# Zero multiplies on TensorE in the front of a gated recurrence with a feed-forward network: more of them, and narrow ones for the remainders

## The chip, the cores and the metric

The kernel runs on one core of one Trainium2 chip. Its time is the device time in microseconds (us) of one execution. Engines: TensorE (PE in the profile; its weight loads are PEld), VectorE (DVE), ScalarE (ACT), GpSimd (POOL), and SyncE (SP), which issues most of the transfers.

## The reference, cut to what matters

A recurrence over 768 steps for 4 batches and 8 heads of width 48, and on its output, 3072 tokens of 384, a feed-forward network with a hidden width of 1536:

```python
f = 1.0 / (1.0 + np.exp(-f_logit))
for t in range(S):
    state = f[:, :, t, :, None] * state + np.einsum('bhd,bhe->bhde', k[:, :, t], v[:, :, t])
    y[:, :, t] = np.einsum('bhd,bhde->bhe', q[:, :, t], state)
...
gate = np.maximum(x @ w_gate, 0.0)
val = x @ w_val
return (gate * val @ w_out).astype(np.float32)
```

## The kernel before

**Tiling.** The tokens are cut into 12 units of 256 (one batch, two chunks of 128). For each unit the kernel takes the logarithm of the gates (ACT, L546 and L555 or L550), sums it along the chunk with a triangle of ones on PE (L562 to L564), forms the exponentials (ACT, L577, L580, L587), multiplies them into k and q (the "hats", DVE or POOL, L599 and L605), transposes these (on PE with L637 for units 0 to 3, by a DMA transpose L648 later), forms the scores (L662), masks them (ptm, DVE L676, or ACT L671 and POOL L673), forms the states (L727 or L717, then DVE L513 and L517, POOL L520) and the output of each chunk (L760, or L767 and L771), and copies that into xT (L402, L403) or by xn and a DMA transpose (L790). L699 and L703 form the total decay of a unit. Two units make a group of 512 tokens; the feed-forward part runs over groups: gate and value (L811, with wg and wv), relu (ACT L816), product (DVE L823), output (L841, with wo), eviction into osb and a store (L862).

**Order.** Nothing is scheduled at run time. `Plan.add` collects the operations ("ops"), numbered in the order in which they are added; `SEQUENCE` gives each engine its order by these numbers, and `HOMES` gives each of the eight PSUM banks the list of tiles that live in it, one after the other. `Plan.needs` works out which semaphores each op waits for, and `run` (L904) writes the waits and the op, engine by engine. An engine works in its order: whatever stands behind a waiting op waits too. POOL issues the weights' transfers (wg, wv, wo in four slices of three hidden blocks each; L482) among its other ops, SP all other ones (loads L468).

**Zeros.** `warm` (L891) is a matmul of a tile of zeros with itself into a bank that is free at that point; its result is read by nobody. `FILLERS` says which op has how many zeros ahead of it and in which bank. They come after those waits of the op which the zeros themselves need (`op.early` of them: the tile of zeros is written, the former tile in that bank has been read by the other engines; L105 to L107) and before the op's other waits:

```python
if n == op.early:
    count, k = FILLERS.get(op.idx, (0, 0))
    for _ in range(count):
        warm(banks[k])
```

So PE multiplies zeros while the release of the op is still to come. All zeros are 512 columns wide (`WARM`). They stand in the first 19 us; the first real matmul behind the nine first ones is the sum of unit 0. The PE ops of the front in their order, with the line of their matmuls and when the first of them starts in the profiled execution:

| op | what | line | starts at, us | zeros before: count |
|---|---|---|---|---|
| 67, 68 | sums, unit 0 | L563, L564 | 6.11 | 9 |
| 105, 106 | sums, unit 1 | L563, L564 | 7.72 | 3 |
| 83 | transposes of k, unit 0 | L637 | 10.03 | 5 |
| 85 | transposes of q, unit 0 | L637 | 10.97 | 1 |
| 123 | transposes of q, unit 1 | L637 | 12.29 | 2 |
| 87, 90 | scores, unit 0 | L662 | 12.84, 13.30 | 0 |
| 121 | transposes of k, unit 1 | L637 | 13.77 | 0 |
| 95 | states, unit 0 | L727 | 14.49 | 0 |
| 128 | scores, unit 1 | L662 | 15.58 | 2 |
| 93 | decay, unit 0 | L699, L703 | 15.91 | 0 |
| 96 | output, unit 0, first chunk | L760 | 16.57 | 0 |
| 125 | scores, unit 1 | L662 | 16.91 | 0 |
| 99 | output, unit 0, second chunk | L760 | 17.56 | 1 |
| 245 | sums, unit 2 | L563, L564 | 18.35 | 1 |
| 132 | decay, unit 1 | L699, L703 | 18.69 | 0 |
| 134 | states, unit 1 | L727 | 19.61 | 2 |
| 135, 244, 138 | output of unit 1, sums of unit 2 between | L760, L563 | 20.05 | 0 |
| 154, then 146 | gates, group 0 | L811 | 21.35, 21.90 | 0 |

The zeros of a row stand ahead of its first op. An output op runs in rounds of four matmuls on a quarter of the array's columns each; scores use 48 of the array's rows.

Of the kernel before, what the change touches and what calls it, by code (L numbers as in the profile page):

```python
# [38 lines left out]
class Plan:  # L39
# [45 lines left out]
    def follow(self, sequence, homes, banks, warm):  # L85
        self.link()
        tiles = list(dict.fromkeys(t for op in self.ops for t in dict.fromkeys(op.reads + op.writes + op.opens) if isinstance(t, Bank)))
        opener = {t: op for op in self.ops for t in op.opens}
        for bank, home in zip(banks, homes):
            before = None  # L90
            for n in home:
                tile = tiles[n]
                tile.ap = bank
                if before is not None:
                    for o in before.ops:
                        opener[tile].deps[o] = "raw" if o.eng == opener[tile].eng == "ACT" else "war"
                before = tile
        assert sorted(n for home in homes for n in home) == list(range(len(tiles)))
        place = {i: n for n, i in enumerate(sequence["PE"])}
        for i, (_, k) in warm.items():  # L100
            op = self.ops[i]
            after = [n for n, t in enumerate(homes[k]) if place.get(opener[tiles[t]].idx, -1) >= place[i]]
            past = [tiles[t] for t in (homes[k][:after[0]] if after else homes[k])]
            assert not past or all(place[o.idx] < place[i] for o in past[-1].ops if o.eng == "PE")
            op.hot = [d for d in op.deps if "zeros" in d.writes] + [o for o in (past[-1].ops if past else []) if o.eng != "PE"]  # L105
            for o in op.hot:
                op.deps.setdefault(o, "war")  # L107
        order = {e: [self.ops[i] for i in sequence[e]] for e in self.ENGINES}
        assert sorted(i for e in self.ENGINES for i in sequence[e]) == list(range(len(self.ops)))
        free = {r: 0.0 for r in self.ENGINES + ("hw", "sw")}  # L110
        at = {e: 0 for e in self.ENGINES}
        left = len(self.ops)
        while left:
            ready = [(max([free[e]] + [d.end for d in order[e][at[e]].deps]), e) for e in self.ENGINES
                     if at[e] < len(order[e]) and all(d.end is not None for d in order[e][at[e]].deps)]
            if not ready:
                raise RuntimeError("the sequences wait for each other")
            start, e = min(ready)
            op = order[e][at[e]]
            op.start, op.pos = start, at[e]  # L120
            free[e] = start + op.occ
            op.end = start + op.occ + op.lat
            if op.flow is not None:
                free[op.ring] = max(free[op.ring], start + op.lat) + op.flow
                op.end = free[op.ring] + 1.0
            at[e] += 1
            left -= 1
        self.order = order
        return order
# [126 lines left out]
        21, 19, 67, 33, 44, 53, 54, 57, 95, 91, 65, 143, 116, 106, 135, 149, 125, 130, 162, 187, 161, 194, 174, 230, 277, 209, 236, 238, 243,  # L256
        271, 260, 263, 292, 298, 301, 314, 316],
]
FILLERS = {67: (9, 0), 105: (3, 0), 83: (5, 0), 85: (1, 0), 123: (2, 3), 128: (2, 7), 99: (1, 2), 245: (1, 2), 134: (2, 3)}

UNITS = {
# [21 lines left out]
def bass_hgrn2_outer__then__ffn_reglu_kernel(  # L283
# [76 lines left out]
    zeros = sb("zeros", [128, 512], BF16)  # L360
    banks = [nc.alloc_psum_tensor(f"ps{i}", [128, 512], F32) for i in range(8)]
# [3 lines left out]
    gp, ve, sc, te, sy = nc.gpsimd, nc.vector, nc.scalar, nc.tensor, nc.sync  # L365
# [79 lines left out]
    WARM = 512  # L445
# [439 lines left out]

    for n in FILLERS:
        pl.ops[n].reads.append("zeros")
    order = pl.follow(SEQUENCE, HOMES, banks, FILLERS)
    waits = pl.needs()

    def warm(bank):  # L891
        return te.matmul(bank[:, 0:WARM], zeros[:, 0:128], zeros[:, 0:WARM], start=True, stop=True, skip_group_check=True)

    sems = {e: nc.alloc_semaphore(f"e_{e}") for e in ("PE", "ACT", "DVE", "POOL")}
    for e in ("PE", "ACT", "DVE", "POOL"):
        n = 0
# [7 lines left out]
    def run(name, eng):  # L904
        for op in order[name]:
            for n, d in enumerate(waits[op] + [None]):
                if n == op.early:
                    count, k = FILLERS.get(op.idx, (0, 0))
                    for _ in range(count):
                        warm(banks[k])  # L910
                if d is None:
                    break
                if d.sem is not None:
                    eng.wait_ge(d.sem, d.goal)
                else:
                    eng.wait_ge(sems[d.eng], d.val)
            ins = op.emit()
            if op.sem is not None:
                ins.then_inc(op.sem, 16)
            elif op.inc:  # L920
                ins.then_inc(sems[name], 1)

    run("SP", nc.sync)
    nc.scalar.preload_act_table_set("natural_log_exp_and_others")
    run("ACT", nc.scalar)
    run("DVE", nc.vector)
    run("POOL", nc.gpsimd)
    run("PE", nc.tensor)
# [30 lines left out]
```

## Time and profile before

| | |
|---|---|
| runs of the kernel, us | 189.0, 189.06, 189.38; median 189.06 |
| the profiled execution, us | 188.75 |
| its span, first to last instruction, us | 187.2 |
| around the span, us | 1.55 |
| busy, share of the span | PE 96%, PEld 55%, DVE 65%, ACT 65%, POOL 56% |

How to read it: a row of the timeline is a start in us from the span's start, the time that the merged instructions cover together, engine, line, operation, what it writes <- what it reads, its shape, and how many were merged. A bracket is idle time before it and what ended it. Each matmul's duration holds the way through the array as well as the streaming of its columns; in a row of several the matmuls overlap, so a second one starts before the first has ended. A row in "rows x columns" such as 128\*32 names the part of the array in use. Some matmul records can be missing.

### The profile page before, as it was taken

The page shows a single profiled execution, that of the slowest core. Times are in us where ns is not written, and L with a number is a line of the kernel's source. Part 1 is how long each engine was busy: PE and PEld are TensorE (multiplying, and loading weights), DVE is VectorE, ACT ScalarE, POOL GpSimd, SP SyncE. Part 2 cuts the span into 40 slices and gives each one's busy share as a digit, 9 for nine tenths or more (in the row PEclk, how much of TensorE's full clock was granted, in tenths as well). Part 3 has the DMA queues.
Part 4 walks back from the last instruction along what each step waited for, and adds up shares of the span by engine and source line. Part 5 has one row for each costly group of instructions (what it writes and reads, how often), then busy time and mean ns, then how long its engine had stood idle before and what let it go on. Part 6 is the DMA issues. An engine that isn't in the chain of part 4 may idle for free.

```text
span 187.2 us, 4314 instructions
## 1 busy us (share of the span) xinstructions
PE 179.2 (96%) x1670; PEld 103.0 (55%) x1691; DVE 121.5 (65%) x231; ACT 122.3 (65%) x242; POOL 104.8 (56%) x141
## 2 busy tenths in 40 slices
PE   7888999999999999999999899999999999999995
PEld 2345686467677555555655355555545465444564
DVE  4099856988179899788679696766744644336151
ACT  3998997999888798879677744463554640545201
POOL 4559905991976999989918989470970700000000
DMA  5999999979899999999999999834544022003005
GB/s 153 324 325 267 209 204 216 279 128 152 185 315 162 226 305 244 224 178 260 254 252 225 252 238 217 189 65 111 166 81 106 30 42 66 0 0 130 17 25 210
DMA packets 83167, 32.89 MB, mean 176 GB/s; under 512 B 75334, under 2 KB 83148, under 8 KB 83148
## 3 DMA queue, kind: packets, MB, share of 16 engines
q1 hardware_dynamic: 78348, 29.09, 64.2%
q0 software_dynamic: 4800, 3.54, 12.8%
q8 instruction: 13, 0.21, 0.5%
q14 instruction: 6, 0.05, 0.1%
HBM read 25.96 MB, written 4.73 MB: 164 GB/s over the span
## 4 chain that ended last, share of the span: by engine, by line
PE 76%; DMA 12%; SPq 4%; POOL 2%; ACT 1%; issue 1%; DVE 1%; ACTq 0%
PE ps L811 44%; PE ps L841 23%; DMA wv<-in_moe_w_val_dram 5%; DMA out_dram<-osb 4%; SPq L468 4%; PE ps L662 3%; DMA v_in<-in_v_dram 3%; PE ps L760 2%; PE ps L771 1%; PE ps L767 1%; PE ps L717 1%; POOL vpad L403 1%; POOL wg L482 1%; PE ps L562 1%; PE ps L727 0%
## 5 line engine op out<-in xcount | busy, mean ns | idle before, releaser
L823 DVE TENSOR_TENSOR gT<-relu,ps 128x512 bf16<-128x512 bf16 (+1 forms) x84 | 50.5, 625 | 31.9 <-PE ps L811 24.0
L816 ACT ACTIVATE relu<-ps 128x512 bf16<-128x512 f32 (+1 forms) x84 | 42.6, 536 | 26.1 <-PE ps L811 19.2
L811 PE MATMUL ps<-xT,wv 128*128 128x512 bf16 (+1 forms) x244 | 54.8, 348 | 1.7 <-DVE osb L403 0.9
L811 PE MATMUL ps<-xT,wg 128*128 128x512 bf16 (+1 forms) x241 | 54.2, 347 | 0.7 <-issue 0.2
L841 PE MATMUL ps<-wo,gT 128*128 128x384 bf16 (+2 forms) x300 | 51.9, 320 | 0.0
L841 PEld LDWEIGHTS ps<-wo,gT 128*128 128x128 bf16 x300 | 28.5, 98 | 18.9
L811 PEld LDWEIGHTS ps<-xT,wv 128*128 128x128 bf16 x252 | 23.3, 98 | 20.6 <-DVE osb L403 1.1
L811 PEld LDWEIGHTS ps<-xT,wg 128*128 128x128 bf16 x252 | 23.2, 98 | 19.4 <-ACT ptm L671 0.4
L673 POOL TENSOR_TENSOR ptm<-ptm,seen 128x512 bf16<-128x512 bf16 x21 | 24.0, 1155 | 15.2 <-ACT ptm L671 14.6
L605 POOL TENSOR_TENSOR hats<-q_in,expo 64x384 bf16<-64x384 f32 x28 | 27.8, 995 | 8.0 <-DMA q_in<-in_q_dram 6.0
L402 ACT ACTIVATE osb<-ps 128x384 f32<-128x384 f32 (+2 forms) x17 | 7.9, 471 | 19.9 <-PE ps L841 18.3
L605 DVE TENSOR_TENSOR hats<-k_in,ps 64x384 bf16<-64x384 f32 x32 | 17.7, 552 | 4.8 <-DMA k_in<-in_k_dram 2.3
L676 DVE TENSOR_TENSOR ptm<-ps,seen 128x512 bf16<-128x512 f32 x27 | 17.7, 682 | 1.7 <-PE ps L662 1.6
L403 POOL CAST vpad<-v_in 64x384 bf16<-64x384 f32 x28 | 14.1, 502 | 6.3 <-DMA v_in<-in_v_dram 5.0
L520 POOL TENSOR_TENSOR st<-ssum,dec 128x384 bf16<-128x384 f32 x16 | 13.3, 831 | 7.6 <-DMA dec<-rates 6.4
L671 ACT ACTIVATE ptm<-ps 128x512 bf16<-128x512 f32 x21 | 11.9, 596 | 7.1 <-PE ps L662 7.1
L546 ACT ACTIVATE f_in<-f_in 128x768 f32<-128x768 f32 x12 | 10.1, 844 | 2.3 <-DMA f_in<-in_f_logit_dram 2.3
L580 ACT ACTIVATE expo<-ps 128x384 f32<-128x384 f32 x22 | 10.0, 490 | 2.5 <-DVE ps L569 2.5
L517 DVE TENSOR_TENSOR ssum<-ps,st 128x384 f32<-128x384 f32 x16 | 8.8, 554 | 3.1 <-PE ps L717 3.0
L587 ACT ACTIVATE ps<-ps 128x384 f32<-128x384 f32 x22 | 10.8, 497 | 0.0
L552 POOL TENSOR_TENSOR bneg<-f_in 128x384 bf16<-128x384 f32 x7 | 7.0, 999 | 4.5 <-ACT f_in L550 4.4
L403 DVE COPY osb<-ps 128x384 f32<-128x384 f32 x8 | 4.4, 553 | 7.0 <-PE ps L841 5.8
(90 smaller groups left out, 175.5 us busy)
## 6 DMA issues: line engine op xcount, KB each, us to landing
f_in<-in_f_logit_dram SPq DMA_DIRECT2D x12, 384.0 KB, 4.9
v_in<-in_v_dram SPq DMA_DIRECT2D x12, 384.0 KB, 4.8
k_in<-in_k_dram SPq DMA_DIRECT2D x12, 384.0 KB, 4.8
q_in<-in_q_dram SPq DMA_DIRECT2D x12, 384.0 KB, 4.8
out_dram<-osb SPq DMA_DIRECT2D x22, 192.0 KB, 2.6
wg<-in_moe_w_gate_dram POOLq DMA_DIRECT2D x4, 288.0 KB, 10.2
wv<-in_moe_w_val_dram POOLq DMA_DIRECT2D x4, 288.0 KB, 9.6
wo<-in_moe_w_out_dram POOLq DMA_DIRECT2D x4, 288.0 KB, 7.5
```

What stands on the lines that cost most here:

```text
L403: return engine[e].tensor_copy(out, src)
L520: add(e, lambda: engine[e].tensor_tensor(t4(s_new), t4(tmp), rate, ALU.mult), [key] + dk, [f"S{b}_{y}"], **(dict(occ=0.79, lat=0.1) if e = ...
L546: add("ACT", lambda: sc.activation(raw["f"], raw["f"], AF.Exp, scale=-1.0), [f"f{li}"], [f"f{li}"], **act_t(2 * HD))
L587: add("ACT", lambda i=i, ex=ex: sc.activation(bc[i].ap[:, 0:HD] if in_place else ex[:, 1, :], bc[i].ap[:, 0:HD], AF.Exp, scale=1.0), [bc[i ...
L605: op = add(e, lambda i=i, n=n, x=x, e=e, y=y, lo=lo, exps=exps: engine[e].tensor_tensor(hats[64 * i:64 * i + 64, hi, y, x, :, 0:D], by_i[n ...
L671: add("ACT", lambda pt=pt, s=sj[j]: sc.activation(pt, s.ap[:, :].rearrange("p (n t) -> p n t", n=NP), AF.Copy), [sj[j]], [f"raw{mis[y]}_{j ...
L673: add("POOL", lambda pt=pt, mask=mask: gp.tensor_tensor(pt, pt, mask, ALU.mult), [f"raw{mis[y]}_{j}", "seen"], [f"raw{mis[y]}_{j}", f"ptm{ ...
L676: add("DVE", lambda pt=pt, mask=mask, s=sj[j]: ve.tensor_tensor(pt, s.ap[:, :].rearrange("p (n t) -> p n t", n=NP), mask, ALU.mult), [sj[j ...
L811: mm = te.matmul(bank.ap[:, 0:n], wt[:, kt, j * 128:(j + 1) * 128], xT[xi][:, kt, n0:n1], start=(kt == 0), stop=(kt == NK - 1))
L816: add("ACT", lambda: sc.activation(relu[ri][:, n0:n1], gate.ap[:, 0:n], AF.Relu), [gate], rk, **act_t(n))
L823: return ve.tensor_tensor(o, a, b, ALU.mult)
L841: mm = te.matmul(bank.ap[:, 0:cut[1] - cut[0]], gT[gi][:, j, r * C:(r + 1) * C], wo[:, j, cut[0]:cut[1]], start=(j == 0), stop=(j == NJ - 1))
```

## The change

Fifteen ops instead of nine have zeros ahead of them, and an entry now has a third number: behind the full zeros (512 columns) comes one narrow zero with that many columns.

```diff
-FILLERS = {67: (9, 0), 105: (3, 0), 83: (5, 0), 85: (1, 0), 123: (2, 3), 128: (2, 7), 99: (1, 2), 245: (1, 2), 134: (2, 3)}
+FILLERS = {67: (10, 0, 0), 105: (4, 0, 0), 83: (5, 0, 448), 85: (2, 0, 0), 123: (3, 3, 192), 87: (0, 3, 192), 90: (0, 7, 384), 121: (0, 7, 320), 95: (0, 7, 384), 128: (2, 7, 384), 96: (0, 4, 320), 99: (1, 2, 256), 245: (2, 2, 192), 134: (2, 3, 320), 146: (0, 5, 256)}
...
-    def warm(bank):
-        return te.matmul(bank[:, 0:WARM], zeros[:, 0:128], zeros[:, 0:WARM], start=True, stop=True, skip_group_check=True)
+    def warm(bank, n=WARM):
+        return te.matmul(bank[:, 0:n], zeros[:, 0:128], zeros[:, 0:n], start=True, stop=True, skip_group_check=True)
...
-                    count, k = FILLERS.get(op.idx, (0, 0))
+                    count, k, rest = FILLERS.get(op.idx, (0, 0, 0))
                     for _ in range(count):
                         warm(banks[k])
+                    if rest:
+                        warm(banks[k], rest)
```

Ops 67, 105, 85, 123 and 245 get one more full zero each; ops 83, 123, 87, 90, 121, 95, 128, 96, 99, 245, 134 and 146 a narrow one. Nothing else is changed: orders, homes and the other engines' work are the same. The zeros of op 146 use bank 5, whose former tile, the state sums of unit 1, is read last by DVE (op 140); those of op 96 use bank 4, whose former tile is read by ACT (op 122).

More of the change, by code (lines that the diff above doesn't have):

```diff
@@ L99, in follow @@
         place = {i: n for n, i in enumerate(sequence["PE"])}
-        for i, (_, k) in warm.items():
+        for i, (_, k, _) in warm.items():
             op = self.ops[i]
```

## The prediction

> **What bounds the kernel now.** I read the page first: where the end comes from.
>
> ```profile
> span 187.2 us, 4314 instructions
> ...
> PE 76%; DMA 12%; SPq 4%; POOL 2%; ACT 1%; issue 1%; DVE 1%; ACTq 0%
> ```
>
> TensorE carries 76% of the chain, so what delays it for good delays the end. The zeros are all in the front, so their line comes next, and then PE's timeline of the front.
>
> ```profile
> L892 PEld LDWEIGHTS ps<-zeros x26: 95/98/152, 1.3 to 18.9; 128*128 128x128 bf16 x26
> L892 PE MATMUL ps<-zeros x24: 376/379/634, 1.7 to 19.1; 128*128 128x512 bf16 x24
> ```
>
> ```profile
> 1.66 4.05 PE L892 MATMUL ps<-zeros 128*128 128x512 bf16 x9
> 6.11 0.34 PE L563 MATMUL ps<-bneg,upto 128*128 128x384 bf16 x1 [0.41 <-ACT bneg L555]
> ...
> 7.72 0.34 PE L563 MATMUL ps<-bneg,upto 128*128 128x384 bf16 x1
> ...
> 8.38 1.24 PE L892 MATMUL ps<-zeros 128*128 128x512 bf16 x5
> 10.03 0.62 PE L637 MATMUL ps<-ident,hats 128*128 128x128 bf16 x8 [0.41 <-DVE hats L599]
> ...
> 10.97 0.62 PE L637 MATMUL ps<-ident,hats 128*128 128x128 bf16 x8
> ...
> 12.29 0.61 PE L637 MATMUL ps<-ident,hats 128*128 128x128 bf16 x8 [0.27 <-DVE hats L599]
> 12.84 0.86 PE L662 MATMUL ps<-qkT 48*128 48x128 bf16 x16
> 13.77 0.62 PE L637 MATMUL ps<-ident,hats 128*128 128x128 bf16 x8
> 14.49 0.21 PE L727 MATMUL ps<-vpad,hats 64*128 64x96 bf16 x1
> ...
> 14.80 0.20 PE L727 MATMUL ps<-vpad,hats 64*128 64x96 bf16 x1
> 15.16 0.38 PE L892 MATMUL ps<-zeros 128*128 128x512 bf16 x1 [0.16 <-issue]
> 15.58 0.40 PE L662 MATMUL ps<-qkT 48*128 48x128 bf16 x8
> ...
> 16.57 0.41 PE L760 MATMUL ps<-ptm,vpad 128*32 128x128 bf16 x16 [0.28 <-DVE ptm L676]
> 16.91 0.40 PE L662 MATMUL ps<-qkT 48*128 48x128 bf16 x8
> 17.24 0.39 PE L892 MATMUL ps<-zeros 128*128 128x512 bf16 x1
> 17.56 0.35 PE L760 MATMUL ps<-qkT,st 128*32 128x128 bf16 x12
> ...
> 18.35 0.34 PE L563 MATMUL ps<-bneg,upto 128*128 128x384 bf16 x1 [0.22 <-ACT bneg L555]
> ...
> 18.92 0.59 PE L892 MATMUL ps<-zeros 128*128 128x512 bf16 x2
> 19.61 0.20 PE L727 MATMUL ps<-vpad,hats 64*128 64x96 bf16 x1
> ```
>
> The clock first. Nine zeros in 4.05 us, the last one 0.63 long, stand 0.427 apart; five from 8.38, the last 0.38 long, stand 0.215 apart. So TensorE is at half speed until 5.07 at least and at full speed from 6.11 on (0.34 for 384 columns), and no zero of the front is slow again: only the ten matmuls up to 5.07 are longer than their width at full speed asks for. Here the pauses do not cool the clock, so the zeros have nothing to win in this execution.
>
> Then who sets the front's end. PE meets the weights of the second slice:
>
> ```profile
> 26.40 1.15 PE L811 MATMUL ps<-xT,wg 128*128 128x256 bf16 x9
> 27.66 0.83 PE L811 MATMUL ps<-xT,wv 128*128 128x256 bf16 x6
> ```
> ```profile
> 17.41 10.20 DMA wv<-in_moe_w_val_dram
> ```
>
> Nine matmuls of 256 columns at 0.11 end their streaming at 27.39; the next starts at 27.66, when wv has landed. So PE has **0.27 us of slack** there. Its transfer is issued by POOL at 17.41 between copies of v that need nothing of PE, so it does not move.
>
> **The change, part by part.** No work is removed. Fifteen places get more zeros. A zero of n columns holds PE n/512 of 0.215: 0.08 for 192, 0.11 for 256, 0.135 for 320, 0.16 for 384, 0.19 for 448. These are estimates by width; between rows, the 256-column matmuls (0.11) and the 384-column ones bear them out.
>
> A second price is in the same rows. Eight L662 from 16.91, in pairs 0.06 apart, are streamed by 17.15, but the zero behind them starts at 17.24; that zero is streamed by 17.456, and op 99 starts at 17.56, though its state was ready at 17.29 (row of 16.73, below). So a change between a full-width zero and a matmul on a part of the array (L662, L727, L760) costs **0.10 each way**. Between a zero and transposes or sums, both full, it costs nothing visible (five zeros from 8.38 follow sums directly).
>
> *Places that fit.* Op 67: the tenth zero, still at 0.427, ends at 5.50 + 0.43 = 5.92, before 6.11. Op 105: sums from 6.11 to 6.77 (four of 0.163), four zeros to 7.63, before 7.72. Op 83: 8.38 + 5 × 0.215 + 0.19 = 9.65, before 10.03. Op 85: eight transposes of 0.056 to 10.48, two zeros to 10.91, before 10.97. Op 123: 11.42 + 3 × 0.215 + 0.08 = 12.15, before 12.29. In all of these the release comes from ACT or DVE later than the zeros; cost nothing, and with that cover gone at most their width.
>
> *Places that don't fit.* Three more rows place ops 90, 154 and 146, and the engines that feed and follow the front are these:
>
> ```profile
> 13.30 0.40 PE L662 MATMUL ps<-qkT 48*128 48x128 bf16 x8
> ```
> ```profile
> 21.35 2.03 PE L811 MATMUL ps<-xT,wg 128*128 128x256 bf16 x15
> ```
> ```profile
> 21.90 1.48 PE L811 MATMUL ps<-xT,wg 128*128 128x256 bf16 x12
> ```
> ```profile
> 13.74 1.29 DVE L676 TENSOR_TENSOR ptm<-ps,seen 128x512 bf16<-128x512 f32 x2
> 15.09 0.11 DVE L430 MEMSET other<- 64x64 bf16 x1
> 15.23 1.29 DVE L676 TENSOR_TENSOR ptm<-ps,seen 128x512 bf16<-128x512 f32 x2
> 16.73 0.56 DVE L513 TENSOR_TENSOR st<-ps,dec 128x384 bf16<-128x384 f32 x1 [0.21 <-ACT dec L708]
> ...
> 20.23 0.56 DVE L513 TENSOR_TENSOR st<-ps,dec 128x384 bf16<-128x384 f32 x1 [0.69 <-PE ps L727]
> ```
> ```profile
> 16.02 0.60 ACT L671 ACTIVATE ptm<-ps 128x512 bf16<-128x512 f32 x1 [0.49 <-PE ps L662]
> ```
> ```profile
> 18.06 0.10 PEld L892 LDWEIGHTS ps<-zeros 128*128 128x128 bf16 x1
> ```
>
> - Op 87: transposes streamed at 12.73, + 0.08 + 0.10 = 12.91, not 12.84: +0.07.
> - Op 90: op 87 ends at 13.08 + 0.07; + 0.10 + 0.16 + 0.10 = 13.51, not 13.30: **+0.20**. DVE's ptm of 13.74 reads its banks and DVE then runs without a pause to 16.52, so everything in it is 0.20 late.
> - Op 121: 13.75 + 0.10 + 0.135 = 13.98, +0.20. Op 95: behind that ptm, +0.20; its 0.16 + 0.10 just fit.
> - Op 128: op 95 ends at 14.84 + 0.20; 0.10 + two zeros 0.43 + 0.16 + 0.10 give 15.83, not 15.58: +0.25. ACT waits for it (idle 0.49 before 16.02), and DVE's state of 16.73 waits for ACT: both +0.25.
> - Op 96: DVE decides, +0.20; its 0.135 + 0.10 fit in the idle 0.28.
> - Op 99: op 125 is streamed at 17.15 + 0.20; 0.10 + 0.215 + 0.11 + 0.10 give 17.87: +0.31.
> - Op 245: the matmul of its one zero is not in the trace (24 of 26 are; the weight load at 18.06 is), so the pause looks emptier than it is. Seven rounds of 0.056 from 17.56 + 0.31 end at 18.28; + 0.095 + 0.43 + 0.08 = 18.89, not 18.35: **+0.54**, and here the zeros themselves are last, since ACT's release is 0.25 late.
> - Op 134: zeros from 18.92 + 0.54, 0.43 + 0.135 + 0.10 behind: 20.12, not 19.61: +0.52. DVE's state of 20.23, which had waited 0.69 for it, op 138 and DVE's later hats move by 0.52.
> - Op 146: the three matmuls of op 154, 0.11 each from 21.35, end at 21.68; a zero of 0.11 fits before 21.90: nothing more, +0.52. The wait that it adds is for a DVE step just ahead of the one that it waits for anyway; behind it in PE's order stand only matmuls that need the same hats.
>
> From 21.90 PE has no pause to 27.39, so that becomes 27.91; wv landed before: 27.91 − 27.66 = **+0.25**, of 0.52 the slack takes 0.27. Ends for the step at each side: with no price for the changes of width only 245's 0.22 is left and the slack swallows it (0); with no slack it is 0.52.
>
> After that, is it given back? PE's one long pause is here:
>
> ```profile
> 107.17 0.59 PE L811 MATMUL ps<-xT,wv 128*128 128x512 bf16 x2 [0.92 <-DVE osb L403]
> ```
> ```profile
> 46.45 1.27 SPq L790 DMA_TRANSPOSE xT<-xn  x1
> ```
> ```profile
> 57.81 4.21 POOL L605 TENSOR_TENSOR hats<-q_in,expo 64x384 bf16<-64x384 f32 x4 [1.79 <-DMA q_in<-in_q_dram]
> ```
>
> That 0.92 could take 0.25, but it is fed by PE itself: SP's loads start behind the transpose of 46.45, which waits for a copy of unit 3's output; the q that ends POOL's 1.79 is one of these loads; SP's later transposes wait for POOL's hats, and the store that frees osb stands in SP's order behind them. So it moves along; I count nothing given back. **Sum: 188.75 + 0.25 = 189.00 for the profiled execution** (span 187.2 and 1.55 around it). The median of the runs is 189.06, 0.31 above that execution; on it I get 189.31, and say 189.3.
>
> **The Trainium skill against the trace.** Rows first: after 6.11 the longest idle bracket of the front is 0.41, and the clock stays full. In "TensorE: Matmul & The Clock Gate", section "Why this matters for your kernels", the skill asks only that no idle gap between bursts is over about 3 us; by that the zeros here have nothing to keep warm, and the sum above stands alone. The same page, section "A second HAM failure mode: psum-queue depth-cycling", tells of short frequent idling between groups that did bring the clock down; by that the front could cool and the change gain, which is rival (4). The trace bears out the first and shows nothing of the second. The page's Part 1 also says that the window which decides is free-running, so that the warm-up point shifts from run to run; one trace cannot show that.
>
> **The rivals.** (1) *Absorbed*: the changes of width are hidden, or the pause at 107 is set by transfers alone and takes all. For: that pause is longer than the loss. Against: the rows around 17.24. Time 189.06. (2) *No slack*: without the profiler wv lands 0.27 or more earlier, PE arrives last anyway, and the whole 0.52 counts: 189.58, slower. Place: 27.66; it decides as soon as wv lands before 27.39. The trace is one execution, and a landing 10.20 after its issue may well differ by 0.27. (3) *Late warm-up*: a run whose clock turns only about 8 us. Sums of op 67 then end at 6.11 + 4 × 0.32 = 7.39, three zeros at 0.427 at 8.67, the fourth at 9.10, against 7.72: +0.43 on top, 189.74. For: the turn lies between 5.07 and 6.11 here by no rule that the trace shows. (4) *The change gains*: other executions do cool in the front and the zeros cure it; the timed runs are 0.31 above the profiled one. A cold stretch as at the start (4.25 us, half lost, pauses and the slack giving back part) would be worth about 1: 188.1. Against: no slow matmul behind 5.07. That the zeros do nothing at all is (1).
>
> **How the numbers follow.** Sum 0.37 (+0.1 to +0.38), absorbed 0.10, no slack 0.24, late warm-up 0.15, gain 0.14. The bound of 0.2% is 0.38 us, about what a measurement of this kernel can tell from no change. Same: 0.37 + 0.10 = 0.47; slower 0.39; faster 0.14. The range goes from 188.7, the median less its distance to the profiled time, to 189.8, above the late warm-up.
>
> **What would show it.** Right: op 90 at 13.51, 128 at 15.83, 99 at 17.87, 245 at 18.89, 134 at 20.12, and the first wv matmul of the second slice at 27.9 behind no pause. Wrong: those ops where they were (no price for width), a pause still before 27.66, zeros at 0.427 behind 6.11, or a shift at 27.9 that is gone at 107.

## The result, and the profile after

The changed kernel takes **190.01 us** (median of 21 runs), the kernel before 189.29 us (21 runs on the same chip); the ratio is 1.0046, 95% interval 1.0024 to 1.0068. By the ratio that is slower by 0.87 us; the medians lie 0.72 apart. Runs more than 1.5% above the fastest of their kernel are left out of every ratio, here one of each (192.27, at a mean granted clock of 0.991, and 191.17). Executions of one and the same kernel lie up to 3 us apart here (before: 187.79 to 191.17), and so one profile can't carry a difference of 0.9 by itself: what follows is read from several profiles of each kind.

The profiled execution took 189.43 us. Three lines of its page, the span, the chain that ended last, and the zeros (busy us, mean ns of one, idle before):

```profile
span 188.1 us, 4369 instructions
...
PE 83%; DMA 7%; DVE 3%; SPq 2%; ACT 1%; POOL 1%; issue 1%; DVEq 0%
...
L892 PE MATMUL ps<-zeros 128*128 128x512 bf16 (+5 forms) x43 | 12.6, 407 | 0.0
```

DMA has 7% of the chain where it had 12%, PE 83% where it had 76%: such shares don't say where 0.9 us went. There are 43 zeros instead of 26, each of them a weight load and a matmul: 34 more instructions on PE. PE's timeline of the front, at the ops that the prediction named:

```profile
6.07 0.34 PE L563 MATMUL ps<-bneg,upto 128*128 128x384 bf16 x1 [0.25 <-ACT bneg L555]
...
13.42 0.40 PE L662 MATMUL ps<-qkT 48*128 48x128 bf16 x8
...
15.75 0.40 PE L662 MATMUL ps<-qkT 48*128 48x128 bf16 x8
...
17.78 0.35 PE L760 MATMUL ps<-qkT,st 128*32 128x128 bf16 x12
...
18.81 0.33 PE L563 MATMUL ps<-bneg,upto 128*128 128x384 bf16 x1
...
20.03 0.21 PE L727 MATMUL ps<-vpad,hats 64*128 64x96 bf16 x1
...
27.81 0.82 PE L811 MATMUL ps<-xT,wv 128*128 128x256 bf16 x6
```

This execution is early already ahead of the first place that doesn't fit: 0.04 us at op 67, 0.08 at op 83 (9.95 instead of 10.03). With 0.08 added, the starts of 13.42, 15.75, 17.78, 18.81 and 20.03 are the forecast 13.51, 15.83, 17.87, 18.89 and 20.12. The front was worked out rightly, and at 27.81 no bracket stands: PE arrives last. The rest of the loss stands far behind the front. First PE at the long pause, then the rows of ACT and DVE that hang on stores there:

```profile
102.42 1.47 PE L811 MATMUL ps<-xT,wg 128*128 128x512 bf16 x6 [0.20 <-DMA xT<-xn]
```
```profile
102.16 0.49 ACT L402 ACTIVATE osb<-ps 128x384 f32<-128x384 f32 x1 [1.51 <-DMA out_dram<-osb]
...
106.11 0.56 DVE L403 COPY osb<-ps 128x384 f32<-128x384 f32 x1 [0.30 <-DMA out_dram<-osb]
```

Before, the same ACT row began 1.00 earlier and had waited less, and PE did not wait for xT at all; its pause came later, at the eviction that follows the second store:

```profile
101.16 0.49 ACT L402 ACTIVATE osb<-ps 128x384 f32<-128x384 f32 x1 [0.86 <-DMA out_dram<-osb]
...
106.33 0.56 DVE L403 COPY osb<-ps 128x384 f32<-128x384 f32 x1 [1.22 <-DMA out_dram<-osb]
```

The second stretch is at 128 to 135, where the load of k lands late; the waits of after between 126 and 137 us (total, times, longest):

```profile
DVE hats L605 <- DMA k_in<-in_k_dram: 1.8, 1, 1.8
...
PE ps L811 <- DVE osb L403: 0.7, 1, 0.7
```

In the first profile of before neither wait is there. Instruction by instruction PE is later in the second profile by 0.43 us at 22 us, 0.34 at 100, 0.0 at 116 to 131 and 0.91 from 134 to the end (DVE by 1.43 at 134). So there were three candidates: the front's lateness, the pause at 100 to 107, and the load at 128.

### The profile page after: what moved, and what is told of

The parts are those of the page before. It is cut to its first block, busy times and chain, and to the rows that moved or that the text cites. A ratio compares the mean times of both kernels' runs of the same rounds, so it can differ in the third digit from the quotient of the medians.

```text
span 188.1 us, 4369 instructions
## 1 busy us (share of the span) xinstructions
PE 183.5 (98%) x1708; PEld 104.2 (55%) x1708; DVE 121.6 (65%) x231; ACT 122.4 (65%) x242; POOL 104.6 (56%) x141
## 4 chain that ended last, share of the span: by engine, by line
PE 83%; DMA 7%; DVE 3%; SPq 2%; ACT 1%; POOL 1%; issue 1%; DVEq 0%
PE ps L811 48%; PE ps L841 20%; PE ps L662 3%; DMA k_in<-in_k_dram 3%; PE ps L760 3%; DMA v_in<-in_v_dram 3%; DMA xT<-xn 2%; PE ps L637 2%; PE ps L892 2%; DVE ptm L676 2%; PE ps L771 1%; SPq L790 1%; PE ps L717 1%; PE ps L767 1%; PE ps L562 1%
## 5 line engine op out<-in xcount | busy, mean ns | idle before, releaser
L811 PE MATMUL ps<-xT,wg 128*128 128x512 bf16 (+1 forms) x252 | 56.2, 349 | 0.9 <-DVE osb L403 0.7
L811 PE MATMUL ps<-xT,wv 128*128 128x512 bf16 (+1 forms) x252 | 56.4, 349 | 0.0
L892 PE MATMUL ps<-zeros 128*128 128x512 bf16 (+5 forms) x43 | 12.6, 407 | 0.0
```

The costliest lines, as they stand in the source:

```text
L811: mm = te.matmul(bank.ap[:, 0:n], wt[:, kt, j * 128:(j + 1) * 128], xT[xi][:, kt, n0:n1], start=(kt == 0), stop=(kt == NK - 1))
L892: return te.matmul(bank[:, 0:n], zeros[:, 0:128], zeros[:, 0:n], start=True, stop=True, skip_group_check=True)
```

## The experiments

**Theories.** (A) *Lateness*: the slack at 27.66 wasn't there, the 0.5 us of the front pass on in full (rival 2). (B) *Absorbed*: the pause swallows it (rival 1). (C) *Moved code*: the longer stream of PE's instructions shifts the transfers that fetch it, and these meet other transfers. (In the expectations of the first four runs, theory C is another one, that the zeros act on the clock; moved code is called theory D from the cut zeros on.) The page of the profile counts 13 transfers of instructions on one queue (q8), 16 KB each, in the span; such a transfer is called a piece below. Before, they start at 88.2, 103.2, 123.1 and 131.8 us and so on; in the changed kernel at 85.1, 99.5, 118.3 and 131.6. They move with PE's instructions: when the piece of 103.2 or 99.5 starts, PE has begun 2228 to 2286 recorded instructions, in each of the twenty profiles of this case. So they are PE's stream, but the count alone doesn't fix the time: with no instruction more than before this piece starts at 103.2 to 105.5 in four profiles, and with 16 more at 103.9 in one kernel and at 99.6 in another. In the Trainium skill, "Runtime: NRT & Kernel Launch", section "Instruction fetch mechanics", a stream is refilled in blocks of 16 KiB, 256 instructions, by a queue of the sequencer's own, at a cost that is "mostly hidden". The sizes agree with this trace; whether the cost is hidden is what (C) puts in question.

Each kernel was run 12 times beside 23 to 35 runs of the kernel before; a ratio stands with its 95% interval. From "The first nine zeros cut into 28" on, an entry of FILLERS is a list of widths and a bank, and the loop runs over the widths.

**Only the five places that fit**, against before:

```diff
-67: (9, 0), 105: (3, 0), 83: (5, 0), 85: (1, 0), 123: (2, 3)
+67: (10, 0, 0), 105: (4, 0, 0), 83: (5, 0, 448), 85: (2, 0, 0), 123: (3, 3, 192)
```


> Only the five places that the prediction called fitting are changed (ops 67, 105, 83, 85, 123 as in the changed kernel; all later zeros as before). Theory A (lateness of PE in the front is what costs): ops 87 to 134 start within 0.1 us of before, first wv matmul of the second slice at 27.66, ratio 1.000. Theory B (any shift of the front changes how transfers fall later, and the end follows these, not PE's lateness): front as before and yet up to 0.9 us longer. Theory C (the zeros act on the clock): no difference either, since no slow matmul was seen behind 5.1 us.

Measured 1.0023 [0.9993, 1.0053]: inconclusive.

**Only the other places**: the change with the five entries above put back.

> The other half: zeros ahead of 67, 105, 83, 85 and 123 as before, all later ones as in the changed kernel. Theory A: the whole loss, ratio 1.004 to 1.005, op 128 at about 15.8, 245 at about 18.9, 134 at about 20.1, the first wv matmul of the second slice at 27.8 to 27.9 without a pause ahead of it. Theory B: the same front, but an end that doesn't follow it, anything from 0 to +0.9 us. Theory C: less than the whole.

Measured 1.0032 [1.0004, 1.006]: clear of no change, but the two intervals overlap, so the pair doesn't say at which places the cost lies.

**The change again**, no edit:

> The changed kernel again, on the chip of the other runs: ratio 1.0046 within its interval of 1.0024 to 1.0068 under every theory; a second profile shows how much of the shift at 27.8 (+0.15), 64 (+0.26) and 107 (none) of the first one repeats. Theory A: the shift at 27.8 stays to the end. Theory B: the shift at 27.8 is the same and that at 107 and 140 another one.

Measured 1.0051 [1.0024, 1.0077]: the first number was no chance.

**Only the first nine zeros**:

```diff
+FILLERS = {67: (9, 0, 0)}
```


> All zeros but the nine ahead of op 67 are left out. Theory A: PE's pauses are empty, no op of the front is later than before, op 99 and what follows a little earlier (0.1 to 0.2); the wv wait at 27.66 takes that: ratio 1.000, at best 0.999. Theory B: anything within 0.9 us. Theory C: the clock drops in the front, matmuls of 128 columns stand 0.107 instead of 0.056 apart, and the time is 1 us or more longer.

Measured 1.0044 [1.0013, 1.0074], with a mean granted clock of 0.964 or 0.973 in all twelve runs. The row of the granted clock (40 slices of 4.7 us) and the transposes of k and q of unit 0:

```profile
PEclk9965599999999999999999999999999999999999
```
```profile
10.20 0.78 PE L637 MATMUL ps<-ident,hats 128*128 128x128 bf16 x8 [1.63 <-DVE hats L599]
11.14 1.04 PE L637 MATMUL ps<-ident,hats 128*128 128x128 bf16 x8 [0.16 <-DVE hats L599]
```

Eight transposes take 1.04 instead of 0.62; the clock's record has half speed from 10.52 to 24.17 us. PE is 2.05 us late at 28 us and 2.07 at the end of this profile, while the runs lose 0.84: how much of a lateness is taken up on the way can't be read from it. So zeros do hold the clock in this front, but those of before already hold it at 1.0, and more can't win. The Trainium skill's "TensorE: Matmul & The Clock Gate", "Why this matters for your kernels", forbids only gaps over about 3 us; here, behind the first zeros, the clock fell with no gap over 1.63, and the measurement decides.

**The first nine zeros cut into 28**: the same time of PE, 38 instructions more.

```diff
-67: ([512] * 9, 0)
+67: ([164] * 28, 0)
```


> The kernel before, with its first nine zeros (9 x 512 columns) cut into 28 of 164: the same columns, 19 more zeros, so 38 more instructions on PE, as many as the change adds; nothing of the front is later. Theory A (PE's lateness in the front costs): ratio 1.000, front as before. Theory D (PE's longer program moves its 16 KB instruction fetches, and one of them then runs beside the load of k at 128 us, which lands 5 us instead of 3.6 us after its issue and holds a store buffer's eviction up): the fetch starts ahead of the end of that load, the load takes about 5 us, ratio 1.003 to 1.005.

Measured 0.9991 [0.9953, 1.0029]: more instructions alone cost nothing that can be seen. That doesn't refute (C): the piece of 103.2 had moved to 96.9, ahead of the place at which it turns out to cost.

**Two zeros less at op 83, two more at op 245**: the front late, the stream as long as before.

```diff
-83: ([512] * 5, 0), 245: ([512], 2)
+83: ([512] * 3, 0), 245: ([512] * 3, 2)
```


> The kernel before with two of the zeros ahead of op 83 put ahead of op 245 instead: the same number of instructions, but op 245 starts about 0.4 us later (18.7 to 18.8), the first wv matmul of the second slice at 27.8. Theory A: +0.15 to +0.4 us, ratio 1.001 to 1.002, and more if lateness is what the change cost. Theory D: the fetch at 131.8 falls as before, the load of k takes 3.6 us in the executions in which it does before; ratio within 0.001 of 1.

Measured 1.0004 [0.9969, 1.0039]; wide, but with no sign of a cost.

**Zeros cut at three places**, 86 instructions more:

```diff
-67: ([512] * 9, 0), 105: ([512] * 3, 0), 83: ([512] * 5, 0)
+67: ([164] * 28, 0), 105: ([128] * 12, 0), 83: ([128] * 20, 0)
```


> The kernel before with the zeros of ops 67, 105 and 83 cut into 28 of 164, 12 of 128 and 20 of 128: the same time in the front, 43 more zeros, 86 more instructions. Theory A: ratio 1.000. Theory D: the fetch moves further ahead, by some 4 to 8 us from 131.8, so to before the load's issue at 128.3; then the load takes 3.6 us again and the ratio is 1.000 or below; if another transfer is met instead, as slow as the change.

Measured 0.9979 [0.9947, 1.0011].

**Before as a kernel of its own**, no edit:

> The kernel before, instruction by instruction, as a kernel of its own: ratio 1.000, which shows what the comparison itself gives; and a second profile of it. Theory A: pauses at 107 and none at 133 as in the first profile. Theory D: the load of k at 128 us and the fetch beside it are a close race (131.77 against a landing at 131.90 in the first profile), so this one may show either 3.6 or 5 us.

Measured 1.0002 [0.9967, 1.0037]. Its profile is the more telling part. PE's chain at the front's end has no wait for wv, and at 132 it has the waits that I had taken for the change's:

```profile
25.86 2.29 PE ps L811 x21
```
```profile
DVE hats L605 <- DMA k_in<-in_k_dram: 1.7, 1, 1.7
...
PE ps L811 <- DVE osb L403: 0.7, 1, 0.7
```

Twenty-one matmuls from 25.86 run on without a pause past 27.33, where this slice of wv is first used; it landed at 26.71. **The slack of 0.27 was one execution's**: in 18 of the 20 profiles PE doesn't wait for it. And a late k belongs to before as well.

**Four and eight full zeros more at op 245**: PE 0.64 and 1.49 us late behind 22 us.

```diff
-245: ([512], 2)
+245: ([512] * 5, 2)
```


> The kernel before with five zeros instead of one ahead of op 245: 0.86 us more of zeros, of which 0.08 fit. Op 245 about 0.8 us later, op 134 and what follows about 0.63 later; weights landed before PE came in the second profile of the kernel before (26.71 against 27.33), so no slack there. Theory A, one to one: +0.63 us, ratio 1.0033. Theory A, amplified as in the change (0.87 us for 0.5 of lateness): 1.0057. Theory B (lateness is swallowed later on): 1.000.

> Nine zeros ahead of op 245: 1.72 us more, op 245 about 1.65 later, op 134 and what follows about 1.5 later. Theory A, one to one: +1.5 us, ratio 1.0079. Amplified: 1.013. Theory B: 1.000; a part swallowed by pauses at 103 to 107 and 133 would give something between, 1.003 to 1.006.

Measured 0.9999 [0.9968, 1.003] for four, 1.0062 [1.0027, 1.0097] for eight (the list 9 long). A lateness like the change's own costs nothing that can be seen; three times as much does. So (A) alone is unlikely.

**The change without its narrow zeros at 87, 90, 121, 95, and 128, 99, 245, 134 as before**; and **the four narrow ones alone**, added to before:

```diff
+87: ([192], 3), 90: ([384], 7), 121: ([320], 7), 95: ([384], 7)
```


> The change repaired: its zeros where they fit (67, 105, 83, 85, 123, and the narrow ones of 96 and 146), the former ones at 128, 99, 245 and 134, none at 87, 90, 121 and 95. PE is nowhere later than before. Theory A: ratio 1.000, first wv matmul of the second slice at 27.3 to 27.7. If zeros gained anything by the clock: below 0.999.

> The kernel before with only the four narrow zeros ahead of ops 87, 90, 121 and 95. Op 90 at 13.5 instead of 13.3, DVE's masks 0.2 later, op 99 at about 17.76; the pauses ahead of 245 and 134 take most of it, so PE leaves the front 0 to 0.1 later. Theory A: ratio 1.000 to 1.0005. If the lateness of DVE and ACT between 13 and 18 us is what costs: 1.001 to 1.003.

Measured 1.0014 [0.9977, 1.005] and 1.0000 [0.9971, 1.003]: neither is clear of no change, and nothing is won.

**The change with its ten first zeros cut into 31**, below the *cut kernel*. The same lateness, 42 instructions more in the stream (21 zeros, each a weight load and a matmul; the expectation counts the zeros alone): this parts (A) from (C).

```diff
-67: ([512] * 10, 0)
+67: ([164] * 31, 0)
```


> The change, with the ten zeros of 512 columns ahead of op 67 in 31 pieces of 164: the same time of PE, 21 instructions more in its stream. Lateness theory: PE comes to the weights of the second slice 0.5 us late as with the change, and the ratio is again near 1.0046 (within 1.002 to 1.007). Theory that the place of the instructions costs: the ratio goes back to about 0.998 to 1.001, as with the pieces alone (0.9991, 0.9979).

Measured **0.9958** [0.9927, 0.999]; the change itself, beside it, 1.0045:

> The change for the third time. Lateness theory with no slack: 1.0025 to 1.005, 0.45 to 0.55 late at 22 us. If its first two ratios (1.0046, 1.0051) were chance on top of the predicted 0.25 us: near 1.0013.

Measured 1.0045 [1.001, 1.0079], for the third time. All twelve runs of the cut kernel (188.12 to 189.46) lie below all twelve of the change beside it (189.62 to 191.57). With one stream of instructions the same zeros cost 0.45%, with another they don't. The front of the cut kernel is as late as the change's, with op 245 at 18.87:

```profile
13.47 0.40 PE L662 MATMUL ps<-qkT 48*128 48x128 bf16 x8
...
17.84 0.35 PE L760 MATMUL ps<-qkT,st 128*32 128x128 bf16 x12
...
18.87 0.33 PE L563 MATMUL ps<-bneg,upto 128*128 128x384 bf16 x1
```

Then the transfers. In the change, a piece of instructions is under way between 99.3 and 101.1 us; the window's row of after, and of the third run of the change (packets, MB, share of 16 engines):

```profile
q8 instruction: 1, 0.02, 3.8%
```
```profile
q8 instruction: 1, 0.02, 3.2%
```

3.8% of 16 engines for 1.8 us is one engine for about 1.1 us. In the same window of before and of the cut kernel there is none; there it stands in the windows 102.5 to 105 and 97.5 to 99.1:

```profile
q8 instruction: 1, 0.02, 2.2%
```
```profile
q8 instruction: 1, 0.02, 3.7%
```

What goes with it there is in PE's and ACT's rows, first of the change in its third run, then in its second:

```profile
103.19 1.47 PE L811 MATMUL ps<-xT,wg 128*128 128x512 bf16 x6 [1.23 <-DMA xT<-xn]
```
```profile
103.03 0.49 ACT L402 ACTIVATE osb<-ps 128x384 f32<-128x384 f32 x1 [2.64 <-DMA out_dram<-osb]
```
```profile
103.81 1.47 PE L811 MATMUL ps<-xT,wg 128*128 128x512 bf16 x6 [1.31 <-DMA xT<-xn]
```
```profile
103.61 0.49 ACT L402 ACTIVATE osb<-ps 128x384 f32<-128x384 f32 x1 [2.69 <-DMA out_dram<-osb]
```

and in the cut kernel, where PE has no bracket between 97 and 110 at all:

```profile
102.19 0.49 ACT L402 ACTIVATE osb<-ps 128x384 f32<-128x384 f32 x1 [0.79 <-DMA out_dram<-osb]
```

For this place in every profile, the table counts the store issued at about 98 us (op 229), from the end of its issue to its landing, and PE's wait for the transposed xT issued next to it:

| profiles | piece starts | store lands after | PE waits for xT |
|---|---|---|---|
| six: the change (4 times, one with the k load moved), only the other places, the change without the narrow ones | 99.5 to 100.5 | 3.60 to 4.34 us | 0.2 to 1.3 us, all six |
| the fourteen others | up to 98.0, or from 103.2 | 1.98 to 2.69 us | none |

The packets say more. Right behind the piece of after (99.48 to 100.58 us) the core's other transfers nearly stop. The first row is after from 100.6 to 101.4, the second before from 99.6 to 100.4, where the same store is under way (packets, MB, share of 16 engines):

```profile
q1 hardware_dynamic: 7, 0.01, 5.8%
```
```profile
q1 hardware_dynamic: 252, 0.19, 82.8%
```

One engine of sixteen would be 6.25%. A landing is told by sixteen steps of a semaphore: of the transpose queued ahead of the store, fifteen come by 100.25 and the last at 101.76, and the store's first comes at 101.88. In the kernel with only the other places these are 101.26, 102.78 and 102.96. In five of the six profiles there is such a stillness between the store's issue and its landing, 1.05 to 1.6 us with 12 packet ends or fewer in any 0.2 us; in the sixth (the change without the narrow ones) and in the fourteen others none is longer than 0.55. In the cut kernel it falls at 98.50 to 99.35, behind the piece of 97.66 and ahead of the end of the store's issue (99.62). Not every piece brings it: behind those of 53.5, 67.0 and 74.8 us in after other packets go on ending, 120 or more in 0.2 us. What decides that stays open.

From 100 to 116 us the six gain lateness against the first profile of before by 0.28 on average (-0.34 to +0.83), the other thirteen lose it by 0.38 (-0.86 to +0.08): 0.66 us apart, with a standard error of about 0.2. The ratios agree: the six stand at 1.0014 to 1.0051, mean 1.0039; the eleven others whose zeros make the front less than a microsecond late at 0.9958 to 1.0023, mean 0.9995.

**The four zeros at 245, with the first nine cut**, and **the later six places alone**:

```diff
-67: ([512] * 9, 0), 245: ([512], 2)
+67: ([164] * 28, 0), 245: ([512] * 5, 2)
```


> Four full zeros more ahead of op 245, and the nine of op 67 in 28 pieces: 0.6 us late at 22 us as with the four alone. Lateness theory: 1.003 (0.6 of 189.5), and the 0.9999 of the four alone was a low sample. Place of the instructions: about 0.998 to 1.000.

> Only the zeros at ops 128, 96, 99, 245, 134 and 146 as in the change, the rest as before. By the prediction's steps op 128 is hardly late, op 99 0.11 and op 245 0.34 late, so PE comes to the second slice about 0.33 late. Lateness theory: 1.0017. If the four narrow ones at 87, 90, 121 and 95 are needed for the cost (they alone gave 1.0000): under 1.001.

Measured 1.0009 [0.9977, 1.004] and 1.0018 [0.9977, 1.006]. Both pass the pause without the wait for xT, and their lateness shrinks there: +1.38 at 100 us becomes +0.64 at 116 in the first, +0.62 becomes +0.06 in the second. That alone doesn't show (B): the four narrow ones alone, without a late front, go from +0.18 to -0.68 at the same place, so the pause differs from one execution to the next. The runs speak for (B): the five kernels whose zeros make the front 0.3 to 0.6 us late and that have no piece at 100 us stand at 0.9958 to 1.0018, mean 0.9998.

**The load of k at 128 moved ahead**, in before and in the change; on SP:

```diff
-921, 775, 821, 780, 782, 826
+921, 782, 775, 821, 780, 826
```


> The kernel before, and on SP the load of k of 128.27 us stands ahead of the transpose of 124.01, where SP has been idle for 2.6 us; its buffer has been free since 79.8, so it can start 6 us earlier, and nothing waits for k at 132. Theory of the load beside the fetch: the executions of the kernel before in which k lands late (as in its second profile, 1.2 us late at 134, 0.8 later at the end) are gone: ratio 0.996 to 0.999 and a narrower scatter, highest run under 190.6. Theory that only the lateness of the front costs: 1.000, scatter as before.

> The change, with the same load moved. Theory of the load beside the fetch: the change loses the 0.9 us by which its profile fell behind between 131 and 137: 1.0045 - 0.0048 = 0.9997, and what is left over the kernel before with the same load moved is the front alone (0.5 us or 0.0026 if it passes on in full, nothing if the pause at 105 takes it). Theory that only the lateness of the front costs: 1.0045 again.

The load's time from issue to landing stood in the window 128 to 129.9 us as follows, in after, in the cut kernel, and in the second and the first profile of before:

```profile
k_in<-in_k_dram SPq DMA_DIRECT2D x1, 384.0 KB, 5.3
```
```profile
k_in<-in_k_dram SPq DMA_DIRECT2D x1, 384.0 KB, 3.8
```
```profile
k_in<-in_k_dram SPq DMA_DIRECT2D x1, 384.0 KB, 5.2
```
```profile
k_in<-in_k_dram SPq DMA_DIRECT2D x1, 384.0 KB, 3.6
```

Before has both times, the change (in three profiles) the long one alone. Measured 0.996 [0.9924, 0.9996] for before with the load moved, 1.0044 [1.0009, 1.0079] for the change. In both profiles DVE's wait for k is gone. Before gains about 0.76 us; the change doesn't gain, against what I expected of it, although its wait is gone as well. So this load is a cost of before, too, and taking it away didn't take away what the change adds; that the change gains nothing at all stays unexplained. (The runs of before beside it spread from 187.92 to 192.29 with a median of 190.17, the change's median is 190.29, so this one ratio hangs on few runs.) At the place of the store, its profile has what the other profiles of the change have:

```profile
103.42 1.47 PE L811 MATMUL ps<-xT,wg 128*128 128x512 bf16 x6 [0.80 <-DMA xT<-xn]
```

**Which theory stands.** What is shown for (C) is that the same zeros with 21 more pairs of instructions lose the cost, and that the slow store and a piece beside it go together in 20 of 20 profiles (a window that was picked after the fact). How much of the 0.87 us arises at that store is less sure. The 0.66 is the distance between profiles with and without the slow store. Between before (three profiles) and the change (four) alone, with the kernels with the moved load of k among them, PE's mean lateness differs by 0.36 us at 99 us, 0.69 at 116 and 0.98 at the end, so by 0.33 in this stretch, and single profiles of the change range there from -0.34 to +0.83. The step from 1.0045 to 0.9958 is 1.65 us, more than this place can give; the cut kernel also has the short load of k. And the one kernel with the slow store and no late front, the change without its narrow zeros, stands at 1.0014, not clear of no change. So the cost is clear where both meet: a late front, which costs nothing visible elsewhere, and a slow store ahead of the pause that would take it up. The split between the two is not shown.

Two versions came out below both kernels: the cut kernel (0.9958 [0.9927, 0.999]) and before with the load of k ahead (0.996 [0.9924, 0.9996]). They were the best of eighteen, which flatters them, and they were not tried together.

## Why the prediction was wrong

It forecast 189.3, +0.25 us, within what can be told from no change; measured were +0.87 on one common chip.

- *The price of widths and of changing them, the places that fit, the ops that don't*: right, within 0.02 us at all five ops that were quoted above, with this execution's 0.08 taken off. No zero behind 6 us was slow in the profile of after, and no clock was won: right as well, and the kernel with only the first nine zeros shows why, since those of before already hold it.
- *"So PE has 0.27 us of slack there"*: wrong. It was the landing of one execution; wv landed at 26.71 in the second profile of before and at 27.08 in that of after, ahead of PE, so the full 0.5 us leave the front. Rival (2) named this, and gave 189.58.
- *"So it moves along; I count nothing given back"*: wrong, the other way, by the runs: five kernels with a late front and no piece at 100 us lose nothing on average (0.9998). The profiles are too uneven to show where it is given back: from 100 to 116 us the six with a late front and no piece give back 0.05 to 0.87, those without a late front -0.08 to 0.86. In the profile of after the shift is gone at 116 us, which the prediction named as a sign of being wrong, and a loss of 0.91 comes back at 134 with the late k. The chain that I argued from, loads behind a transpose behind PE, is there but isn't what ends the pause: in before, a copy ends it that waited 1.22 us for a store (the row of 106.33 above).
- **The step that failed** is the first sentence of the change part by part: "No work is removed. Fifteen places get more zeros." I costed the zeros only as time on PE and put their instructions at nothing, without a reason. The 34 instructions that they add moved the piece that was fetched at 103.2 us to 99.5, where it meets a store and a transpose that PE waits for: profiles with that meeting lose 0.66 us against the others there, and with the same zeros in another stream the ratio is 0.9958 instead of 1.0045. How the 0.87 divides between this and the two steps above stays open.
- *The rivals*: slower was right, by none of their mechanisms alone: rival (2)'s lateness leaves the front, without a piece at 100 us it is taken up as in rival (1), and with one a wait that no rival had comes on top. The late turn of rival (3) does occur, but isn't what costs here: in the change with the k load moved the first sum takes 0.50 us instead of 0.34, and with the first nine zeros only the clock's record is full from 7.10 us; in the change's other three profiles the first sum takes 0.34.

## What to carry to other kernels

Instructions that do nothing still have to be fetched: when a long straight program gets more of them, look where the transfers of its code fall against the loads and stores that the bound engine waits for, far behind the place of the edit. Before a small slack or a small gain is believed, take a second profile of the same kernel. And when a change costs something, run it once with the same work in another number of instructions, which tells whether the cost lies in the work or in its place in the stream: here that took the ratio from 1.0045 to 0.9958.

## What the runs showed of the hardware

- Where a transfer of 16 KB of instructions (one packet of 0.9 to 1.4 us) starts 0.7 to 1.5 us behind the issue of a store of 192 KB, the store lands 3.60 to 4.34 us behind that issue instead of 1.98 to 2.69, and the transpose queued next to it lands just behind the store. In five of these six profiles the core's other packets nearly stop for 1.05 to 1.6 us (7 packets from 100.6 to 101.4 us in after).
- The load of k at 128 us took 4.9 to 5.8 us from its issue in thirteen profiles, and in eleven of these it landed 1.96 or 1.97 us behind the start of a piece (2.07 and 2.70 in the others), whenever that was; the pieces of the eleven took 0.92 to 0.96 us, so the load lands about 1 us behind a piece's end. In twelve of the thirteen, one of the sixteen steps of the load's semaphore comes 1.27 us or more ahead of the other fifteen (132.11 and 133.38 in after); in the first profile of before all sixteen come within 0.20. It took 3.6 to 4.2 us in the five where a piece started with the issue's end or before, or as late as the landing or later.
- The clock fell to a mean of 0.964 or 0.973 over the execution, in all twelve runs, with PE's pauses behind the first zeros no longer than 1.63 us in the profile, in a front in which 26 zeros instead of nine kept it at 1.0.
